# Moving the four narrow output jobs behind all wide ones

## The chip, the cores and the metric

One core of one Trainium2 chip. The metric is device microseconds for one execution of the program, median of several; lower is better.

## The reference

A causal attention with a forgetting factor (8 batches, 8 heads, 576 rows, 64 columns a head), and behind it a spectral layer: the first 64 Fourier modes along the sequence are multiplied by complex 512 x 512 weights, transformed back, and added to their input; the result `u` goes through a last matrix.

```python
y = np.fft.irfft(Y, n=S, axis=1)
u = x + y
return (u + np.maximum(u @ w_ch, 0.0)).astype(np.float32)   # 8 x 576 x 512, f32
```

576 rows are four blocks of 128 and one of 64. Those last 64 rows are what the change is about.

## The kernel before

The last stage computes, for each block of rows, two sums in PSUM: `pu` (that is u) and `pz` (that is u @ w_ch). ScalarE copies `pu` to SBUF, VectorE makes `max(pz, 0) + u`, and SyncE sends the result to DRAM. The work is cut into 20 jobs. Jobs 0 to 3 take two row blocks of one batch each; twelve *wide* jobs take the same block of two batches; four *narrow* jobs take the last 64 rows of two batches, one batch in partitions 0 to 63, the other in 64 to 127.

```python
jobs = []
for b in range(0, B, 2):
    if b == 0:
        jobs += [((c, sb), (c, sb + 1)) for c in (b, b + 1) for sb in (0, 2)]
    else:
        jobs += [((b, sb), (b + 1, sb)) for sb in range(4)]
    jobs.append(((b, 4),))
...
for n, job in enumerate(jobs):              # cut: the first jobs, order of the matmuls
    ...
    emit_u(jobs[n + 1], nxt, uo_n[0])       # ScalarE: u <- pu of the next job  (L1014)
    emit_o(job, ps, *uo, n == 0)            # VectorE and the DMA of this job

def emit_o(job, ps, u, o, pair, split=False):               # cut
    nc.vector.scalar_tensor_tensor(                         # L1019
        o[:, bs, :], ps[1][:, bs, :], 0.0, u[:, bs, :], ALU.max, ALU.add)
    b, sb = job[0]
    n_wide = 4 * (b // 2 - 1) + sb
    if sb == 4:                                             # narrow: two DMAs of 128 KB
        for h in range(2):
            nc.sync.dma_start(                              # L1026
                out[b + h, 512:576, :], o[64 * h : 64 * h + 64, 0, :])
    elif not wide(job):
        nc.sync.dma_start(...)                              # L1030: jobs 0 to 3
    elif sb % 2 or n_wide < 2:                              # wide: two DMAs of 512 KB after
        for j, (bj, _) in enumerate(job):                   # each second job (the first two
            nc.sync.dma_start(...)                          # jobs: 256 KB each at once; L1039)
```

The softmax here doesn't subtract the row's maximum and nothing guards it: scores larger than these inputs give would overflow.

## Time and profile before

| | before |
|---|---|
| median | 436.08 us (436.05 to 436.23, 3 runs) |
| span of the profiled run | 434.3 us |
| last weights reach VectorE (last add at L156) | 399.78 us |
| output | first issue 404.01 us, packets 405.17 to 432.69 us, 9.44 MB |
| VectorE's last job | ends 426.18 us |

A row of the page's table has 40 digits, tenths of busy time in 40 equal slices. Where this text tells of single packets, they are the trace's own DMA packets; it has queue, start, duration and size of each, but not which of the 16 DMA engines carried it. Where one engine is followed below, that is done by the times: its next packet begins just before its previous one ends, mostly by 3 or 4 ns (in the packets followed back from the end of the kernel before, below).

### The profile page before, as it was taken

To read this page: it belongs to the slowest core of one execution; us is meant where nothing else is said; L and a number is where in the kernel's file an instruction comes from. 1 tells how busy PE (TensorE), PEld (TensorE's weight loads), DVE (VectorE), ACT (ScalarE), POOL (GpSimd) and SP (SyncE) were. 2 spreads that over 40 slices of the span, in tenths; PEclk is the share of its full clock that TensorE was granted. 3 is DMA by queue.
4 is the path that set the end of the run, shared out by engine and by line. 5 is a ranking of instruction groups with operands and counts; after the bars stand their busy time and mean duration, and the time that the engine had idled before them with its cause. 6 is when DMAs were issued, how large, how long until landed. Compare 5 with 4: busy or idle time off the path is not lost.

```text
span 434.3 us, 12369 instructions
## 1 busy us (share of the span) xinstructions
PE 358.8 (83%) x5328; PEld 247.5 (57%) x5346; DVE 264.4 (61%) x659; ACT 225.0 (52%) x339; POOL 126.8 (29%) x198
## 2 busy tenths in 40 slices
PE   3787799999987978878778797799999977888881
PEld 2454566776665756666656565666665544554540
DVE  5797888876465665556566577524324654653892
ACT  2888488774526446364464554143443443731771
POOL 8333332223232232332323322232222322200400
PEclk9996899996557868577597779599999999999997
DMA  8999999999999999999999999999999999996697
GB/s 181 235 235 239 236 237 238 246 212 217 228 220 237 220 229 233 215 237 227 222 236 212 213 211 211 211 211 211 211 211 211 211 211 211 211 212 127 240 383 272
DMA packets 51086, 97.39 MB, mean 224 GB/s; under 512 B 3799, under 2 KB 12983, under 8 KB 51031
## 3 DMA queue, kind: packets, MB, share of 16 engines
q0 software_dynamic: 46464, 85.65, 101.0%
q1 hardware_dynamic: 4567, 10.95, 7.1%
q8 instruction: 42, 0.69, 0.6%
q14 instruction: 13, 0.11, 0.1%
HBM read 163.73 MB, written 9.44 MB: 399 GB/s over the span
## 4 chain that ended last, share of the span: by engine, by line
PE 33%; DMA 27%; ACT 11%; DVE 11%; issue 5%; DVEq 0%; POOL 0%; ACTq 0%; SPq 0%
DMA wb<-in_moe_w_i_dram 26%; ACT E L590 8%; PE pav L628 7%; PE A L191 6%; PE ps L583 6%; PE tp L321 5%; PE vp L555 3%; PE px L671 2%; DVE QTs L336 2%; ACT KT L334 2%; DVE x_all L650 1%; DVE os L1019 1%; PE pz L842 1%; DVE XT L685 1%; DVE E L605 1%
## 5 line engine op out<-in xcount | busy, mean ns | idle before, releaser
L590 ACT ACTIVATE E<-ps 128x1024 bf16<-128x1024 f32 (+1 forms) x128 | 101.3, 849 | 28.2 <-PE pav L628 17.2
L191 PE MATMUL A<-XT,wb 128*128 128x16 bf16 x1984 | 71.9, 181 | 12.0 <-DMA wb<-in_moe_w_i_dram 7.0
L191 PEld LDWEIGHTS <-wb 128*128 128x128 bf16 x1984 | 64.1, 100 | 27.5 <-issue 13.2
L96 POOL DMA_DIRECT2D wb<-in_moe_w_r_dram x64 | 42.7, 667 | 123.6 <-PE A L191 24.7
L583 PE MATMUL ps<-QTs,KT 64*128 64x64 bf16 (+4 forms) x384 | 55.8, 320 | 14.5 <-ACT E L590 12.4
L96 POOL DMA_DIRECT2D wb<-in_moe_w_i_dram x64 | 42.3, 660 | 81.7 <-DMA wb<-in_moe_w_i_dram 38.1
L628 PE MATMUL pav<-va,E 128*128 128x65 bf16 (+1 forms) x1088 | 53.6, 205 | 7.1 <-DVE x_all L650 6.5
L628 PEld LDWEIGHTS <-E 128*128 128x128 bf16 (+1 forms) x1088 | 43.6, 111 | 17.2 <-DVE x_all L650 8.9
L605 DVE TENSOR_TENSOR E<-E,trimask 128x256 bf16<-128x256 bf16 (+2 forms) x128 | 37.0, 304 | 19.5 <-ACT E L590 18.8
L881 ACT CAST XW<-pxw 128x512 bf16<-128x512 f32 x36 | 20.7, 587 | 35.6 <-PE pxw L874 23.4
L340 ACT COPY VT<-tp 128x640 bf16<-128x640 bf16 (+1 forms) x32 | 23.1, 759 | 28.3 <-PE tp L321 28.3
L583 PEld LDWEIGHTS <-KT 64*128 64x128 bf16 x384 | 19.1, 99 | 31.4 <-issue 20.8
L334 ACT COPY KT<-tp 128x640 bf16<-128x640 bf16 (+1 forms) x32 | 22.0, 751 | 26.0 <-PE tp L321 25.8
L924 ACT CAST XW<-pB 128x512 bf16<-128x512 f32 x36 | 21.1, 586 | 26.7 <-PE pB L842 26.6
L874 PE MATMUL pxw<-wch,yy 128*128 128x512 bf16 x133 | 33.6, 385 | 1.1 <-issue 0.5
L923 DVE CAST x_all<-pA 128x512 bf16<-128x512 f32 x36 | 24.9, 692 | 12.5 <-PE pA L842 10.6
L336 DVE COPY QTs<-tp 128x640 bf16<-128x640 bf16 (+1 forms) x32 | 23.4, 768 | 14.2 <-PE tp L321 14.0
L650 DVE TENSOR_TENSOR x_all<-pav,rcp 128x384 bf16<-128x384 f32 x64 | 29.1, 455 | 1.1
L639 DVE RECIPROCAL rcp<-pav 128x6 f32<-128x6 f32 x64 | 12.1, 189 | 24.5 <-PE pav L628 23.6
L156 DVE TENSOR_TENSOR YTe<-A,Yacc 128x128 bf16<-128x128 f32 x16 | 5.9, 368 | 33.1 <-PE A L191 33.1
L555 PE MATMUL vp<-ident_bf,VT 128*128 128x128 bf16 x205 | 21.4, 256 | 4.5 <-DVE QTs L336 3.8
L842 PEld LDWEIGHTS <-ident_bf 64*64 64x64 bf16 (+1 forms) x336 | 15.1, 107 | 17.0 <-issue 8.2
(142 smaller groups left out, 610.8 us busy)
## 6 DMA issues: line engine op xcount, KB each, us to landing
wb<-in_moe_w_r_dram POOLq DMA_DIRECT2D x62, 512.0 KB, 16.7
wb<-in_moe_w_i_dram POOLq DMA_DIRECT2D x62, 512.0 KB, 17.4
stv<-in_v_dram POOLq DMA_DIRECT2D x9, 576.0 KB, 15.6
out_dram<-os SPq DMA_DIRECT2D x10, 512.0 KB, 4.8
stk<-in_k_dram POOLq DMA_DIRECT2D x11, 288.0 KB, 15.6
stq<-in_q_dram POOLq DMA_DIRECT2D x11, 288.0 KB, 15.4
wx<-in_v_dram POOLq DMA_DIRECT2D x5, 576.0 KB, 16.2
out_dram<-uo SPq DMA_DIRECT2D x3, 512.0 KB, 4.2
```

The lines of the kernel that those rows point to most:

```text
L96: keep(nc.gpsimd.dma_start(dst, src))
L191: ins = nc.tensor.matmul(A[:, eb, mi, :], lhsT=w_of(mi, eb * 128), rhs=x_of(m), start=(i == 0), stop=(i == len(terms) - 1),)
L334: nc.scalar.copy(rows(KTs[pr % 2][:, :, 0:S]), tv)
L336: ins = nc.vector.tensor_copy(rows(QT[pr][:, :, :]), tv)
L555: nc.tensor.transpose(vp[:, sc, :, :].rearrange("p b d -> p (b d)"), VTs[s // 2 % 2][:, h, sc * 128 : (sc + 1) * 128], ident_bf[:, :],)
L583: nc.tensor.matmul(ps[:, b, o : o + n], lhsT=KTs[pr % 2][bs, h, jb * 128 : (jb + 1) * 128], rhs=QT[pr][bs, h, jb * 128 + c0 : jb * 128 + c ...
L590: nc.scalar.activation(E[:, :, piece * 512 : piece * 512 + w], ps[:, :, 0:w], ACT.Exp, scale=scale,)
L605: nc.vector.tensor_tensor(dg, dg, tr, ALU.mult)
L628: nc.tensor.matmul(pav[64 * half : 64 * half + w, slot, :], lhsT=E[:, b, c : c + (w - 1) * st + 1 : st], rhs=va[:, jb, b, :], start=(n == ...
L650: nc.vector.tensor_tensor(xo, pi, ri, ALU.mult)
L874: nc.tensor.matmul(pxw[:, :], lhsT=xT[:, eb, i * 128 : (i + 1) * 128], rhs=wch[:, eb, :], start=(eb == 0), stop=(eb == NDC - 1),)
L923: nc.vector.tensor_copy(xs, pA[:, :])
```

## The change

The intent: let the wide jobs run without interruption, and finish with small jobs whose transfers are short.

```diff
             else:
                 jobs += [((b, sb), (b + 1, sb)) for sb in range(4)]
-            jobs.append(((b, 4),))
+        jobs += [((b, 4),) for b in range(0, B, 2)]
         ps = start(0)
```

## The prediction

> **What bounds the kernel now.** The change touches only the last stage, so I first asked the page where that stage lies. Three rows of its table of 40 slices (10.86 us each):
>
> ```profile
> DVE  5797888876465665556566577524324654653892
> DMA  8999999999999999999999999999999999996697
> GB/s 181 235 235 239 236 237 238 246 212 217 228 220 237 220 229 233 215 237 227 222 236 212 213 211 211 211 211 211 211 211 211 211 211 211 211 212 127 240 383 272
> ```
>
> From slice 2 to 36 the DMA engines are 90% busy or more: the weights stream in, and the chain of waits is "DMA wb<-in_moe_w_i_dram" for most of 284 to 399 us. The last three slices (about 401.7 us on) are the output stage: 240, 383 and 272 GB/s. All jobs that the change reorders run there, so I cut that stage by the narrow jobs (columns: stretch in us, its length, busy us of each engine, granted clock, DMA share, GB/s):
>
> ```profile
> 404.00:409.10 5.10, 4.32 (x60) 2.63 (x60) 4.70 (x5) 3.52 (x4) 2.44 (x6) 1.00 0.78 276
> 409.10:415.30 6.20, 5.28 (x88) 3.01 (x83) 5.64 (x6) 4.44 (x5) 0.00 (x0) 1.00 0.95 341
> 415.30:421.30 6.00, 5.08 (x84) 2.94 (x80) 5.61 (x6) 4.69 (x6) 0.00 (x0) 1.00 1.01 381
> 421.30:427.50 6.20, 3.29 (x44) 1.24 (x36) 4.67 (x5) 3.28 (x4) 0.00 (x0) 1.00 1.01 376
> 427.50:434.30 6.80, 0.00 (x0) 0.00 (x0) 0.00 (x0) 0.00 (x0) 0.00 (x0) 0.59 0.60 220
> ```
>
> Two things are near their limit: VectorE (third busy number, 5.6 of 6.0 us) and the DMA engines (share 1.01). Which one sets the end? VectorE stops at 426.18, the DMA goes on for over 6 us. So the compute is ahead, and the end is set by the output DMA: when it starts, how often it runs dry, and how fast it goes. The chain of waits names "DVE os" up to 425.6; I read past it, because nothing on VectorE can be the last link 8 us before the end.
>
> The transfers in one-microsecond slices from 395 to 435 us, and the issues behind them (KB each, median us to landing):
>
> ```profile
> GB/s 188 161 134 63 33 3 16 33 53 62 285 272 352 398 414 391 207 299 369 367 401 404 381 268 412 401 414 410 401 236 381 412 410 414 401 277 170 16 8 0
> ...
> out_dram<-os SPq DMA_DIRECT2D x10, 512.0 KB, 4.8
> ...
> out_dram<-uo SPq DMA_DIRECT2D x8, 128.0 KB, 4.2
> ```
>
> The plateau is 401 to 414 GB/s; it has holes at 411, 418, 424 and 430 us. The SyncE queue, which issues every output transfer, tells what they are (start, us, line, number):
>
> ```profile
> 409.11 2.07 SPq L1026 DMA_DIRECT2D out_dram<-uo  x2
> 411.28 3.93 SPq L1039 DMA_DIRECT2D out_dram<-os  x6
> 415.30 2.29 SPq L1026 DMA_DIRECT2D out_dram<-uo  x2
> 417.69 3.48 SPq L1039 DMA_DIRECT2D out_dram<-os  x4
> 421.26 2.54 SPq L1026 DMA_DIRECT2D out_dram<-uo  x2
> 423.90 3.52 SPq L1039 DMA_DIRECT2D out_dram<-os  x4
> 427.54 2.48 SPq L1026 DMA_DIRECT2D out_dram<-uo  x2
> ```
>
> L1026 is the narrow job: two DMAs of 64 partitions each. Each hole comes about 2 us after such a pair. Read one by one, the trace's packets of 2 KB took 117 to 126 ns in the first DMA of each pair, against 85 to 87 ns for the 2 KB packets of 128-partition DMAs at L1039.
>
> [...] (the first packet of a pair's second DMA comes 0.73 to 1.18 us after that of its first). [...] here 1.59 us pass from the last output packet (432.69) to the end of the span (434.28).
>
> **The change, part by part.** It removes and adds no work. The two compiled programs have the same instructions on every engine, in another order, and differ only in this stage: after the five DMAs at L1030, SyncE now issues 4 + 10 transfers of wide jobs and then 8 narrow ones; VectorE does 12 wide jobs, then 4 narrow ones.
>
> *Compute.* A wide job costs VectorE about 1.22 us (three back to back: 410.70 to 414.18, 1.16 each), a narrow one 0.68. The first wide job after a narrow one starts 0.87 us after it and lasts 1.43 us to the next start, for want of ScalarE's copy; three of these hitches go away, some 0.3 us each. But VectorE is ahead of the DMA (12 x 1.16 us a job against 1.29 us a job for its transfer), so that buys nothing.
>
> *Start of the wide stretch.* Job 3 leaves VectorE at 408.49 in both. Then wide job k should leave at 408.5 + 1.16k. In the kernel before, the gap in DMA supply here was filled by the first narrow pair, issued at 409.11. Now the first wide transfers go out at about 409.75, while job 3's own data still runs (first packet 409.85, then 1.28 us). Four transfers of 256 KB follow, 0.72 us from first packet to first packet (412.56, 413.28, 414.01, 414.73 before): 411.1, 411.8, 412.55, 413.25. They would be used up at 414.0. From there on, a transfer goes out only after each second wide job: jobs 3 and 4 are done at 413.15, the issue takes 0.5, and the first packet came 0.62 us after the issue's end when the queue was empty (404.55 to 405.17). So the first 512 KB transfer starts at 414.3, with a new hole of 0.3 us, and 0.95 us ahead of its 415.25 before.
>
> *Wide stretch.* Ten transfers of 512 KB took, first packet to first packet, 2.65 + 5.13 + 5.14 = 12.92 us before (415.25 to 417.90, 418.94 to 424.07, 425.11 to 430.25). 414.3 + 12.9 = 427.2 for the first narrow packet. That compute keeps up: jobs 5 and 6 are done at 415.5, their turn comes at 416.9.
>
> *Narrow tail.* A pair costs 1.04 us to the next first packet (417.90 to 418.94, 424.07 to 425.11), and some 0.15 to 0.25 us more that show in the next wide transfer (1.42 and 1.54 us instead of 1.28), because an engine lags: 1.2 us is my estimate. Three of them are moved from the middle to the end, not saved. The last pair took 430.25 to 432.69, 2.44 us to its last packet. 427.2 + 3 x 1.2 + 2.44 = 433.2, against 432.69. With the same 1.59 us behind it the span gets 0.5 us longer: 436.08 + 0.5 = 436.6.
>
> In one sum: bytes, packets and narrow pairs are conserved; the new hole at 414 us costs 0.3 us, and the rest is rounding between measured intervals.
>
> **Rivals.** *First, issue time becomes the bound.* Narrow issues took SyncE 0.54 to 1.48 us (median 1.17), wide ones 0.33 to 0.54 mostly. Were that the narrow DMA's own price, eight at the end would take 8 x 1.2 = 9.8 us after the last wide issue at about 424.3, would end at 434.1 instead of 430.03, and give 440 us. Against it: the very first narrow issue took 0.54, behind few transfers, and every long one ends shortly before the transfer two places ahead of it runs out (issue ends 417.59, 423.81, 430.03; the first narrow packets follow at 417.90, 424.07, 430.25). So SyncE is held by the queue: it looks as if little over two DMAs fit, whatever their size. Then a narrow tail holds just 256 KB in the queue, some 1.1 us of work, against about 0.6 to 1.1 us from issue to first packet: tight, and it could cost 1 to 2 us. This is the weightiest rival, and pulls my range upward.
>
> *Second, narrow neighbours help each other.* [...] A pair at the plateau's rate would take 0.64 us; at 8 x 0.45 us (a short issue and its gap) the tail would be done about 1 us sooner: 435.5. The mean of 88 to 101 ns in three of the pairs' second DMAs speaks a little for it.
>
> *Third, buffers.* Output tiles turn round in a ring of nine. In the new order each of the last tiles follows one whose transfer was issued some 6 us or more before, against landing times of 4 to 5 us; the 0.4 us that ScalarE now waits for "DMA out_dram<-uo" at 418.77 would vanish. No effect on the end, as ScalarE isn't what the DMA waits for.
>
> *Fourth, the lag of one engine builds up* over eight narrow transfers. If it grew by 0.5 us with each pair, the end would be 1.5 us later, 438. Against it, the queue's short depth makes the others wait for the slow one[...].
>
> **Range and chances.** Every term here is a fraction of a microsecond, and 2% is 8.7 us: more than the whole narrow tail. Only the first rival in its full strength comes half way. Runs of the kernel before agree within 0.2 us. So 436.6, with 435.2 (rival two) to 438.2 (rivals one or four in part); faster by over 2%: 0.01, within 2%: 0.97, slower by over 2%: 0.02.
>
> **What would show it.** In the changed profile: everything up to about 401 us as before; VectorE's wide jobs without a gap over 0.3 us, done near 422.5 and its last narrow one near 426; one hole in the GB/s row near 414 us, then the 401 to 414 plateau without holes to about 427; then some 5 us at 200 to 270 GB/s. Narrow issues of about 0.6 us each would confirm the held queue; 1.2 us each with idle DMA engines between would confirm the first rival. A narrow tail at 350 GB/s or more would confirm the second. The prediction is wrong if the span changes by more than 2 us, or if the first narrow packet comes far from 427 us.

Where a cut is marked, the prediction gave reasons that no trace or run of this case shows: why 64 neighbouring partitions are slow to read and why the DMAs of a pair follow one another, in rival two why neighbours would help each other, and in rival four what a slow engine gains from the others' waiting. 427.2 + 3 x 1.2 + 2.44 = 433.2, which is 0.5 us after 432.69, and with the measured 1.59 us behind it 436.08 + 0.5 = 436.6. What carries the sum are the times: 117 to 126 ns for a narrow pair's first packets against 85 to 87, and 0.73 to 1.18 us from the first packet of one DMA of a pair to that of the other. That little over two DMAs fit in the queue is the prediction's own reading of the issue times that it lists.

## The result, and the profile after

| | before | after |
|---|---|---|
| median | 436.06 us (435.78 to 436.84, 6 runs) | 435.94 us (435.19 to 436.24, 6 runs) |
| ratio | | 0.9992, 95% interval 0.9979 to 1.0005 |
| last add at L156 starts | 399.78 | 400.40 |
| job 3 leaves VectorE | 408.49 | 409.14 |
| last output packet | 432.69 | 432.72 |

A ratio is the mean time of one kernel's runs over that of the other's of the same rounds, so not quite the ratio of the medians. Note the rows below it: in the profiled run the new order got its weights 0.6 us later, and ended at the same moment. Such a shift in the weight stream, hundreds of microseconds long, is as large as anything the change does. So I compare the stage by itself.

The rows of the page that answer to those shown before (VectorE, DMA, GB/s):

```profile
DVE  5797888876465665556566577624324654653891
DMA  9999999999999999999999999999999999996798
GB/s 185 233 236 240 235 236 238 247 212 218 227 221 235 223 226 234 214 236 229 220 235 213 213 210 211 211 211 211 211 211 211 211 211 211 211 211 122 257 384 255
```

Up to the output stage no slice of this table tells the two kernels apart; in its last three slices the changed kernel moves a little more at first (257 GB/s instead of 240) and less at the end (255 instead of 272). The stage cut as before (stretch, length, busy us of PE, PEld, DVE, ACT, POOL, clock, DMA share, GB/s):

```profile
404.00:409.10 5.10, 4.74 (x62) 2.62 (x59) 4.69 (x6) 3.73 (x5) 3.06 (x7) 1.00 0.77 266
409.10:415.30 6.20, 5.59 (x88) 2.88 (x91) 6.18 (x7) 5.20 (x6) 0.00 (x0) 1.00 0.94 360
415.30:421.30 6.00, 5.59 (x90) 2.80 (x84) 6.00 (x6) 5.32 (x6) 0.00 (x0) 1.00 1.02 404
421.30:427.50 6.20, 3.55 (x35) 1.20 (x28) 4.25 (x6) 2.74 (x5) 0.00 (x0) 1.00 1.03 402
427.50:434.30 6.80, 0.00 (x0) 0.00 (x0) 0.00 (x0) 0.00 (x0) 0.00 (x0) 0.60 0.68 169
```

VectorE is now busy all the time from 409 to 421 us (6.18 of 6.20, 6.00 of 6.00), and the rate from 415 to 427 is 404 and 402 GB/s instead of 381 and 376. All of it is given back after 427.5 us: 169 GB/s instead of 220. VectorE's and SyncE's own rows (start, us):

```profile
409.05 13.91 DVE L1019 SCALAR_TENSOR_TENSOR os<-pz,us 128x1024 f32<-128x1024 f32 x12
422.87 0.68 DVE L1019 SCALAR_TENSOR_TENSOR uo<-pz,uo 128x512 f32<-128x512 f32 x1
423.72 1.30 DVE L1019 SCALAR_TENSOR_TENSOR uo<-pz,uo 128x512 f32<-128x512 f32 x2 [0.17 <-ACT uo L1014]
425.18 0.69 DVE L1019 SCALAR_TENSOR_TENSOR uo<-pz,uo 128x512 f32<-128x512 f32 x1 [0.15 <-PE pz L842]
```

```profile
410.29 14.60 SPq L1039 DMA_DIRECT2D out_dram<-os  x14
424.99 6.31 SPq L1026 DMA_DIRECT2D out_dram<-uo  x8
```

Twelve wide jobs took 13.91 us, 1.16 each, and VectorE stopped at 425.87, 0.3 us before its old time, though it had begun 0.65 us later. The transfers in slices of 1 us from 395 us on, and their issues:

```profile
GB/s 169 139 108 48 44 16 33 16 44 55 209 340 352 348 410 414 371 367 381 221 393 410 397 426 393 406 410 397 393 401 414 397 340 238 223 219 207 125 0 0
...
out_dram<-os SPq DMA_DIRECT2D x10, 512.0 KB, 4.9
...
out_dram<-uo SPq DMA_DIRECT2D x8, 128.0 KB, 2.7
```

There is one hole, at 414 us (221 GB/s), then 393 to 426 GB/s up to and with 426, 340 at 427 and four slices of 207 to 238. The prediction had said nearly that. The durations of the narrow issues (ns: least, median, most), before and after:

```profile
L1026 SPq DMA_DIRECT2D out_dram<-uo x8: 537/1168/1481, 409.1 to 428.6; - x8
```

```profile
L1026 SPq DMA_DIRECT2D out_dram<-uo x8: 518/588/1231, 425.0 to 430.7; - x8
```

So the long issues of before weren't the price of a narrow DMA: in the new order six of the eight took 0.52 to 0.60 us, and the two right behind the wide transfers 1.19 and 1.23. I take what is over 0.60 us as waiting in the queue.

The last 8 us in slices of 0.2 us from 427 us, first the kernel before, then the changed one, show what I had missed:

```profile
DMA  9999999999999999996987511000000010000000
GB/s 369 471 389 369 451 410 389 430 389 451 369 451 369 430 389 410 348 236 174 215 277 266 195 72 41 20 31 20 10 0 0 0 41 0 0 0 0 0 0 0
```

```profile
DMA  9998977899789888987996998996010000000000
GB/s 389 430 318 246 317 205 184 246 266 287 215 236 277 195 195 215 256 195 195 236 236 174 215 205 205 215 205 143 21 41 0 0 0 0 0 0 0 0 0 0
```

Before, the rate is down to 72 GB/s at 431.6 and goes on at 10 to 41 for another microsecond: one engine is still working, alone. The trace's last packets then end 0.08 us apart, one at a time, up to 432.69, while the other engines were done by 432.0. After, the rate stays at about 200 until 432.4 and all engines stop within 0.2 us.

### The profile page after: what moved, and what is told of

Its sections match the earlier page's. It is cut to its first block, busy times and chain, and to the rows that moved or that the text cites. A ratio compares the mean times of both kernels' runs of the same rounds, so it can differ in the third digit from the quotient of the medians.

```text
span 434.3 us, 12362 instructions
## 1 busy us (share of the span) xinstructions
PE 360.1 (83%) x5328; PEld 247.1 (57%) x5346; DVE 264.5 (61%) x659; ACT 225.4 (52%) x339; POOL 127.1 (29%) x198
## 4 chain that ended last, share of the span: by engine, by line
PE 34%; DMA 26%; ACT 12%; DVE 11%; issue 5%; POOL 0%; ACTq 0%; DVEq 0%
DMA wb<-in_moe_w_i_dram 26%; ACT E L590 8%; PE pav L628 7%; PE A L191 6%; PE ps L583 6%; PE tp L321 5%; PE vp L555 3%; PE px L671 2%; DVE QTs L336 2%; ACT KT L334 2%; PE pz L842 1%; DVE XT L685 1%; DVE os L1019 1%; PE pu L842 1%; DVE x_all L650 1%
## 5 line engine op out<-in xcount | busy, mean ns | idle before, releaser
L156 DVE TENSOR_TENSOR YTe<-A,Yacc 128x128 bf16<-128x128 f32 x16 | 5.9, 368 | 33.1 <-PE A L191 33.1
```

## The experiments

I measure the stage from the start of the last add at L156 to the last output packet; it needs no clean start of the weights. First values: 32.91 us before, 32.32 after. Theory A: the stage is bound by the output DMA, and the narrow transfers are slow because of which partitions they read, 64 neighbouring ones (117 to 126 ns for a packet of 2 KB in the first DMA of a pair, against 85 to 87 from 128 partitions). The rivals B, C and E, and a theory D formed after the first four runs (one engine falls behind because it also has to carry a 16 KB packet of the kind that the trace calls "instruction"), are in the expectations; what led to theory D is told under the second of these runs.

### The same kernel again

No edit.

> The changed kernel once more, for a second profile and a tighter interval. I measure the output stage by itself: from the end of VectorE's fifth job at L1030 to the last output packet. First profiles: 24.20 us before, 23.58 after, while that job ended 0.65 us later in the second. Theory A (the stage is bound by the output DMA, and the new order saves some 0.6 us of it; the later start is run-to-run noise of the weight stream): stage again 23.4 to 23.8 us, time 435.4 to 436.0, ratio 0.998 to 1.000. Rival (the stage is as long as before and the 0.6 us were chance): stage 24.0 to 24.4, ratio 1.000 or above.

Measured: 436.21 us (435.33 to 436.35, 6 runs) against 436.05, ratio 1.0003 (0.9988 to 1.0017). Job 3 left VectorE at 408.93 and the last packet came at 432.70: 23.77 us, within theory A's range. The ratio was the rival's (1.000 or above), and the time too long for theory A. Together with the first comparison: no difference in time can be shown, in either direction, beyond some 0.2%.

### Striped narrow transfers, new order

```diff
-  out[b + h, 512:576, :], o[64 * h : 64 * h + 64, 0, :]
+  out[b + h, 512:576, :], o[h:128:2, 0, :]
```

> Wrong result on purpose (rows of the two batches are mixed): each narrow DMA of the changed kernel reads every second partition instead of one half of the partitions; bytes, count and rows of 2 KB are the same. Theory A[...]: the 2 KB packets at L1026 fall from 116-154 ns to 85-92 ns; the tail from the first narrow packet, 5.16 us, becomes bound by SyncE's issues (8 x 0.6 us), so 4.6 to 4.8 us, time 435.5. Rival B (they are slow because they are small, or by a price for each DMA): packets stay above 115 ns, tail 5.1 to 5.3 us, time 435.9.

What the run tests is whether the choice of the partitions makes the packets slow.

Measured: 435.42 us, ratio 0.9990 (0.9976 to 1.0004). The narrow packets took 84 to 86 ns in the mean of a DMA, instead of 118 to 148. The tail took 4.67 us from its first packet (427.44 to 432.11), and SyncE issued one DMA after the other (0.59 us each in the median, from 424.7 to 430.4). Rival B is out: it is the choice of partitions and not the size that makes the packets slow. The tail becomes bound by the issues instead, as expected, and so little is gained from packets that take about a third less time.

### Striped narrow transfers, old order

The same edit on the kernel before.

> Wrong result on purpose, the same edit on the kernel before. Theory A: the holes at 411, 418, 424 and 430 us go, a pair takes about 0.7 us instead of 1.04 to 1.2 from first packet to next first packet, so 4 x 0.4 to 0.5 us less: 434.1 to 434.6 us, ratio 0.996. Here the issues aren't back to back, so they don't bind. Rival B: packets above 115 ns, holes stay, 436.0.

Measured: 435.59 us, ratio 0.9990 (0.9976 to 1.0004), so a third of what I expected, or less. The packets did fall, to 85 to 94 ns, and two of the pairs took 0.7 us. Why is so little gained? The last 8 us from 427 us, as above:

```profile
DMA  9999999999999998998111100000000100000000
GB/s 389 410 369 451 430 369 430 430 348 410 430 430 389 451 369 307 369 348 338 62 41 72 41 20 31 20 31 0 0 0 0 41 0 0 0 0 0 0 0 0
```

From about 431 us on the digits are 1: one or two engines out of 16 are busy, with 20 to 70 GB/s. Fourteen engines were done by 431.0, one more by 431.65, and the last packet came at 432.49. So what the narrow packets cost (88 to 126 ns in the mean of a DMA in the kernel before, 85 to 94 striped) had mostly been paid by engines that had to wait for a slow one anyway.

What makes one engine slow? The packet list has on queue 8, of kind "instruction", packets of 16 KB that took 0.89 to 1.48 us each over all profiles; in the first profile of before at 401.33, 413.40 and 425.09 us. They seem to be TensorE's: the whole execution has 42 of them, and TensorE ran 10,674 instructions, 254 for each packet in the mean (169 to 347 between neighbours); between those three packets it ran 280 and 275, every other engine fewer than 35. (With 144 instructions added to TensorE, a packet came at 409.10 us instead of 413.65: see the shift below.) I take such a packet to occupy one DMA engine for its 0.89 to 1.48 us, while each output transfer is dealt out to the 16 in equal shares; that is read from the times, as below, where eight of 128 packets come late. The transfer whose first packet came at 414.73, just after the 16 KB packet of 413.40 to 414.43, ended 0.97 us later than its first 90% of packets; the three before it had ended 0.06 to 0.12 us later. That is theory D: one engine falls behind by about 1 us and sets the end.

The packets' times show that it is the same engine. Followed back from the last packet of the kernel before, 56 packets lead without a gap from 432.69 to 425.999 us, where the 16 KB packet of 425.09 to 426.01 ends. In that narrow pair the link rests on no choice: 120 of its 128 packets had ended by 425.68, and the eight that were left, one engine's share, came one after the other from 425.999 on. In the other profiles that end on one late engine (the second of the kernel before, stripes and shift on the old order, narrow first with and without the shift) the same walk leads to a 16 KB packet as well, but there it has to choose between packets with nearly the same times. In five profiles (before twice, stripes on the old order, narrow first with and without the shift) the last packet came 1.1 to 1.6 us after the median of the last 16 completion packets, as I call those of 4 bytes of which the trace has 16 for each output transfer.

### The narrow jobs first

```diff
                 jobs += [((c, sb), (c, sb + 1)) for c in (b, b + 1) for sb in (0, 2)]
+                jobs += [((n, 4),) for n in range(0, B, 2)]
             else:
                 jobs += [((b, sb), (b + 1, sb)) for sb in range(4)]
-        jobs += [((b, 4),) for b in range(0, B, 2)]
```

> All four narrow jobs ahead of the wide ones, correct result. Theory A (a pair costs some 1.2 us wherever it stands; what order changes are the new hole before the first 512 KB transfers, 0.4 us, and the lag at the end, up to 1 us): no hole after the narrow pairs, because the wide jobs get ahead while the DMA works them off, and no narrow pair at the end: stage 23.0 to 23.6 us, time 435.3 to 435.9. Rival C (order matters by more than that: narrow jobs first starve the DMA, as each pair gives only 256 KB per VectorE job of 0.7 to 0.9 us): stage over 24.5 us, time 436.5 or more.

Measured: 437.78 us, ratio 1.0042 (1.0028 to 1.0056), stage 34.42 us. The prediction of theory A failed, and though the time is rival C's, its reason isn't: VectorE was through with all narrow jobs long before their transfers were.

```profile
409.33 1.29 DVE L1019 SCALAR_TENSOR_TENSOR uo<-pz,uo 128x512 f32<-128x512 f32 x2 [0.17 <-issue]
410.79 0.69 DVE L1019 SCALAR_TENSOR_TENSOR uo<-pz,uo 128x512 f32<-128x512 f32 x1 [0.17 <-PE pz L842]
411.40 1.23 DVE L1019 SCALAR_TENSOR_TENSOR os<-pz,us 128x1024 f32<-128x1024 f32 x1
```

The transfers, in slices of 1 us from 395 us:

```profile
GB/s 164 152 99 51 16 33 32 34 49 63 269 297 326 406 401 401 227 246 236 158 84 207 354 385 402 401 401 401 414 381 397 414 414 397 410 397 410 295 37 4
```

The rate falls to 158 and 84 GB/s at 414 and 415 us. A 16 KB packet ran from 413.65 to 414.67; SyncE's seventh narrow issue was held 1.40 us (413.64 to 415.04), and the sixth transfer's last packet came 1.1 us after its median one, where the others had 0.3 to 0.4. If the queue takes little over two DMAs, as the prediction read from the issues, two narrow ones hold 256 KB, and the other 15 engines ran dry behind one; that is my reading of the 84 GB/s and of the held issue. And at the end the last packet came at 434.27, the other engines' by 433.0. This is where theory D got its test.

### Shifting the instruction packets

```diff
-  for i in range(nb):
+  for i in [j for j in range(nb) for _ in range(3 if eb == 0 else 1)]:
       nc.tensor.transpose(ptr[...], x_all[...], ident_bf[:, :])     # in emit_xw
```

Some transposes are made three times, about 100 us ahead of the stage; 144 instructions more on TensorE, the result is the same.

> Correct result. The kernel with the narrow jobs first, and 72 transposes more on TensorE some 100 us earlier (144 instructions, about half of what seems to lie between two 16 KB instruction packets), to shift the moments of those packets. In the unshifted one the packet at 413.65 us hit the narrow transfers: SyncE's seventh narrow issue was held 1.40 us, the rate fell to 84 GB/s, stage 34.42. Theory D: the packets come at about 406 to 409 and 418 to 421 us, the hold of 1.4 us and the hole of 84 GB/s are gone, stage 33.2 to 33.7, time 436.6 to 437.2; the engine that carried the later packet still ends about 1 us after the others. Rival E (holes and lag come from the order of the transfers alone): stage 34.2 to 34.6, time 437.8 as before the shift, or later by what the added instructions cost.

Measured: 437.07 us, ratio to before 1.0016 (1.0002 to 1.0029, just touching that of the unshifted one), stage 33.54 us. The packets came at 409.10 and 419.17 us. SyncE's rows of the eight narrow issues, unshifted, then shifted:

```profile
409.18 6.50 SPq L1026 DMA_DIRECT2D out_dram<-uo  x8
```

```profile
409.60 5.85 SPq L1026 DMA_DIRECT2D out_dram<-uo  x8
```

The rate in the shifted one, from 395 us:

```profile
GB/s 176 174 125 53 23 16 0 16 63 52 280 302 369 323 397 378 225 217 215 209 211 230 371 379 401 383 408 418 393 406 410 406 410 414 397 414 401 201 20 0
```

The hold and the hole of 84 GB/s are gone (issues 2 to 8 took 0.54 to 0.59 us, the rate stays at 209 to 230), the transfer under way at 419.17 got the lag instead (its last packet came 1.6 us after its 90%), and the last packet of all came 1.1 us after the bulk. Stage, hold and lag are as theory D had them (the first packet just outside the expected 406 to 409 us), and rival E is out. The 15 other engines needed 32.5 us from the last add, as in the changed kernel: the order cost them nothing.

### The shift on the two kernels of the case

The same edit on each.

> Correct result. The kernel before with the same 72 transposes more some 100 us earlier, so that the 16 KB instruction packets come at about 408.5 and 420 us instead of 413.4 and 425.1. Theory D: one engine is still behind at the end, by 0.5 to 1.2 us, because the two narrow pairs that follow give it back only in part; stage 32.4 to 33.0, time 435.8 to 436.3. [...]

> Correct result, the same shift on the changed kernel. Theory D: the packets come at about 409 and 419 us; whichever engine lags, the eight narrow transfers at the end give it time to catch up: all 16 engines end within 0.2 us of each other, stage 32.2 to 32.6, time 435.7 to 436.2. If the even end were a matter of when the packets come, one engine would be 0.8 us or more behind and the stage 33.0 or more.

The rival said: if the lag is due to the narrow pairs and not to the 16 KB packets, stage and lag are as in the unshifted kernel to 0.1 us.

Measured: 435.98 us for the old order (0.9993, 0.9980 to 1.0005), 435.95 for the new one (0.9990, 0.9978 to 1.0002). In the new order all engines ended within 0.2 us, as expected. In the old one the last packet came 0.25 us after the other engines' (0.56 after the median of the last 16 completion packets; 1.07 without the shift), less than I expected. The last 8 us from 427 us, old order, then new:

```profile
GB/s 451 369 389 451 451 369 369 451 430 389 369 512 389 348 369 492 389 389 369 328 256 195 256 266 277 164 51 20 10 0 0 0 41 0 0 0 0 0 0 0
```

```profile
GB/s 348 471 471 369 328 277 246 225 297 379 277 318 205 236 246 256 215 205 236 236 195 225 246 184 174 256 215 174 31 0 41 0 0 0 0 0 0 0 0 0
```

Both stages were shorter than expected (31.87 and 31.93 us): just one 16 KB packet came after 410 us instead of two. So the rival of the first expectation, a stage as in the unshifted kernel to 0.1 us, is out, and with the packets shifted the two orders need the same stage. The old order gains 0.8 to 1.0 us by the shift, the new one 0.4 to 0.6: the packets cost the new order something too, inside its plateau or at the passage to the narrow tail; where, is left open.

### The kernel before again

No edit.

> The kernel before once more, for a second profile of it. Stage from VectorE's last add at L156 to the last output packet: theory D says 32.7 to 33.1 us as in its first profile (32.91), with one engine 0.8 to 1.3 us behind the other 15 at the end; the changed kernel gave 32.31 and 32.51 with none behind. Rival (the difference was chance): stage 32.2 to 32.6. Time 436.0 to 436.2, ratio 1.000.

Measured: 436.82 us (435.77 to 437.86) against 436.43 of the same kernel beside it, ratio 1.0010 (0.9997 to 1.0023): that is the noise. Stage 32.63 us, just under the expected range and just over the rival's; the bulk was done by 432.28, the last packet came at 433.23, 0.95 us later, as expected. The two profiles of the new order gave 32.32 and 32.51. So the new order shortens the stage by some 0.1 to 0.6 us, less than the spread of the times; four profiles are few, and what separates the orders clearly is the late engine at the end (about 1 us behind in both profiles of the old order, level in both of the new).

### Two queues

```diff
-  nc.sync.dma_start(
+  (nc.sync, nc.scalar)[h].dma_start(
       out[b + h, 512:576, :], o[64 * h : 64 * h + 64, 0, :])
```

> Correct result. The changed kernel with the second DMA of each narrow job issued from ScalarE's queue instead of SyncE's, so that [...]SyncE issues only four. I now measure the stage from the start of VectorE's last add at L156 to the last output packet: 32.91 us before, 32.32 and 32.51 after. Theory A alone[...]: 8 narrow transfers in about 2.9 us instead of 5.2, stage 30.2, time 433.9, ratio 0.995. Theory D (one of the 16 engines is some 1.2 us behind after it has carried a 16 KB instruction packet of about 1 us, and sets the end when the narrow tail doesn't give it time to catch up): the other 15 engines are done about 430.8, the last one alone near 432.0, stage 31.6 to 32.0, time 435.2 to 435.6.

> Correct result, the same edit on the kernel before. Theory A alone: the holes go, 4 x 0.5 us less: stage 30.9, time 434.1. Theory D: as with the striped source (stage 32.2, 15 engines done 1.5 us before the last one), so stage 31.9 to 32.4, time 435.4 to 435.8. ScalarE has to wait for VectorE before each of its DMAs[...].

In the first, a reason for the edit and a gloss on theory A are cut; the 2.9 us there is an estimate, near 4 x 0.72 us, what four transfers of 256 KB took before from first packet to first packet. In the second, a cost of ScalarE's waiting is cut that was worked out from no run.

Measured: 436.08 us on the new order (0.9995, 0.9983 to 1.0008), 437.28 on the old (1.0024, 1.0012 to 1.0037). On the new order the stage was 32.00 us, so at the edge of theory D's range and far from theory A's 30.2. But theory D's number came out without its reason: the other engines were done at 432.0 instead of 430.8, and the last one just 0.3 us later. And the time didn't follow: from the last packet to the end it took 2.05 us instead of 1.6. The GB/s from 395 us:

```profile
GB/s 165 148 107 54 25 27 45 19 35 66 117 316 327 400 406 401 387 363 385 311 406 401 401 422 393 410 418 406 397 385 401 250 373 318 305 285 205 6 8 0
```

ScalarE's halves, issued ahead, mixed with wide transfers from 426 us on (there their packets took about 170 ns, the rate fell to 250). In the slices at 429 and 430 us, where almost nothing wide is left, the halves ran at 305 and 285 GB/s, where the one queue had 207 to 238. On the old order both theories missed: stage 33.21 us. Half transfers stood beside wide ones in four places (packets of 85 to 205 ns in the mean of a DMA), and SyncE was held 1.85 us before its last one. I didn't take this apart further.

### A finer start

```diff
-  elif sb % 2 or n_wide < 2:
-      rs = slice(sb % 2 if n_wide < 2 else 0, sb % 2 + 1)
+  elif sb % 2 or n_wide < 4:
+      rs = slice(sb % 2 if n_wide < 4 else 0, sb % 2 + 1)
```

> Correct result. The changed kernel with the third and fourth wide job sent out job by job (four transfers of 256 KB instead of two of 512 KB after the fourth), which takes away the hole near 414 us. By my recorded sum the hole costs 0.3 to 0.4 us[...]: stage 0.2 to 0.3 us shorter, 32.1, time 435.7 to 435.9. By theory D the hole may cost nothing, as the lagging engine is the one that matters, or as the narrow tail gives back what is gained: stage 32.3 to 32.5.

Cut is a price for the smaller rows that was worked out from no run; the 0.2 to 0.3 us is what it left of the 0.3 to 0.4 us of the hole.

Measured: 435.57 us (435.32 to 436.45), ratio 0.9992 (0.9979 to 1.0004). The hole at 414 us was gone (348 GB/s there), but the rate fell to 268 a slice later, behind a 16 KB packet from 413.63 to 414.59 and an issue held 1.25 us. The profiled run was the slowest of the five (436.45), with a stage of 32.95 us: there SyncE's last narrow issue waited from 430.95 to 431.40. In the trace of the changed kernel SyncE's output DMAs carry eight semaphores in turn (108, 109 and 113 to 118), and the last narrow issue waits for 113, which the last wide DMA has. Here that one's slowest engine had ended at 429.77, 1.6 us before the issue was let go. No gain can be shown.

No version beats both kernels by more than 0.15%. A layout in which striped narrow rows are right was not built.

## Why the prediction was right or wrong

436.6 us was predicted, within 2%; 435.94 was measured, in the range of 435.2 to 438.2. That the two are so close says little: the six runs of the kernel before spread over 1.06 us, where the prediction had taken 0.2 us from three. The steps, counted from the moment job 3 leaves VectorE:

| step | predicted | after | again |
|---|---|---|---|
| to the first 512 KB transfer | 5.81 | 5.49 | 5.48 |
| ten transfers of 512 KB | 12.9 | 12.93 | 13.02 |
| three narrow pairs | 3.6 | 3.76 | 3.85 |
| last pair, to its last packet | 2.44 | 1.40 | 1.42 |
| sum | 24.7 | 23.58 | 23.77 |

- *Compute is ahead and buys nothing*: right. VectorE did its wide jobs in 1.16 us each without hitches, and the time stayed.
- *A new hole*: right, 0.39 us (413.52 to 414.63, less 0.72), and 0.28 in the second profile. It came a little earlier after job 3 than predicted, as the issue took 0.33 us and not 0.5.
- *Wide stretch and pairs are conserved*: right, to 0.25 us.
- *The last pair takes 2.44 us as before*: wrong by 1.04 us. I took it for the price of a pair. The runs show that about 1 us of it was the lag of one engine, waited for at the end; the eight narrow transfers of the new order, paced by issues of 0.52 to 0.60 us and packets of 118 to 148 ns, let it catch up. The trace of the changed kernel shows this too: after the 16 KB packet of 424.20 to 425.26 one engine ended the tenth 512 KB transfer at 429.36, 1.34 us after nine tenths of it were done. It then needed 0.33 us for its share of each narrow transfer, where the others took about 0.64 us for each, and was level with them at the sixth. The last pair of the old order is two such transfers, and gives back only about 0.6 us. The prediction did have a lagging engine in its sum, with 0.15 to 0.25 us for each pair, but not at the end. So the sum "+0.5 us" had the wrong sign: -0.6 us in the first pair of profiles, between -0.1 and -0.6 over all four.
- *First rival, issue time*: refuted as to its size, right as to the argument against it. Issues took 0.59 us in the median and were held only behind wide transfers (1.19 and 1.23 us).
- *Second rival, neighbours help each other*: not in either profile of this order (118 to 148 ns throughout); that it is the choice of partitions which makes the packets slow is shown by the stripes (84 to 86 ns). Its sum was wrong besides: eight transfers of 0.45 us take 3.6 us, and the tail of the main sum takes 6.0, so it should have said 2.4 us sooner and not 1, and the range's lower end was too high for it.
- *Third rival, buffers*: right; ScalarE's wait of 0.4 us for an output DMA is gone from the changed profile.
- *Fourth rival, a lag that builds up*: the opposite (1.34 us at the tenth 512 KB transfer, none at the sixth narrow one); but a lagging engine is what I should have looked for in the profile of before, where it stood in the rates that the prediction shows (16 GB/s at 432 us).
- *Smaller slips*: 8 x 1.2 is 9.6 and not 9.8, which changes nothing. "The same instructions on every engine" holds for the work; the changed program has seven semaphore waits fewer (12,362 instructions against 12,369). The 1.59 us behind the last packet that the sum takes from the trace were 1.60 after.

So the verdict was right for the reason given (bytes, packets and narrow pairs are conserved in a stage that the DMA bounds); one term was mis-sized, and it decided the sign of a difference that the times can't resolve. That the lag comes from the instruction packets rests on the shift and on the packets followed back from the end; the trace doesn't name the engine, so which packets are one engine's is read from their times.

## What to carry to other kernels

In this stage, bound by the DMA, reordering the jobs moved the holes around and nearly kept their sum. In such a case look at what is last in the queue, and whether the last bytes come from all 16 engines or from one. A slice table of the last few microseconds shows this at once: in the kernel before it had 10 to 41 GB/s after 431.6 us, with the packets ending one at a time, and a sixteenth of the plateau would be 410 / 16, about 26 GB/s (an estimate for one of the 16 engines alone). Small transfers in a row proved fragile: with narrow jobs first, one late engine held an issue for 1.40 us and the rate fell to 84 GB/s.
